# Block 1's statistics behind block 0's scaling, turns' copies ahead of others, and six drains in the prologue

## The chip, the core and the metric

One core of a Trainium2 chip. Times are device microseconds (us) of a whole execution. Each kernel was run several times in rounds, each round beside the kernel before on the same chip; a profile is one further execution, whose span (first to last instruction) is 1.6 to 1.8 us below the timed figure.

## The reference, cut to what matters

```python
x = A_x                                   # 2048 tokens x 512, bf16
xn = layernorm(x)                         # over the 512, no gain, no bias
qkv = xn @ wqkv                           # 32 heads of 16
a = softmax(mask(q k^T / 4)) v            # causal, window of 256 keys
out = x + a @ wo + ((xn @ w_gate) * (xn @ w_up)) @ w_down
```

The tokens are worked in four chunks of 512, a chunk in four blocks of 128. The scores are the matmuls of q k^T; PE does them in 76 batches, and the exponentials of the softmax follow on ACT. Of the work, only that of chunk 0, the first 17 us, is touched.

## The kernel before: what the change and the argument touch

The kernel is written out by a list scheduler of its own: while it is built, it simulates the engines with a table of durations and emits each instruction when its turn comes. V is DVE, A is ACT, G is POOL, P is PE. Cuts are marked.

```python
class Kernel:
    HOLD = 0.1
    # ... prologue: loads, constants, then
        nc.gpsimd.memset(self.V[0][:, :, :, 16:18], 1.0)
        self.keep_busy(42, 0)             # 42 dummy matmuls on PE

    def loop(self):                       # the next copy, scaling, ...
        # ... for every waiting op o and every engine e that may do it
        key = (at + (0.3 if e == "A" and len(o.on) > 1 else 0.0)
               + (self.HOLD if o.rank and now0 else 0.0), o.rank, t)
        # ... the smallest key is done next; now0: no score batch yet

    def choose(self):                     # the next work of PE
        # ... for the first four dense pieces d, t = when it could start
        t -= 0.3 * (d.name.startswith("turn") and t <= now + 0.25)
        # ... the smallest t wins

    def first_chunk(self):
        land = (3.4, 3.95, 7.7, 9.6)      # landings of x, blocks 0 to 3
        wv, wk, wq = 5.9, 7.3, 9.3        # landings of the weights
        # per block b: statistics (DVE), root (ACT), reciprocal and scaling (DVE),
        # "turn": four transposes on PE and a copy xT out of PSUM (rank 0),
        # then V, K, Q projections (16 matmuls each) and copies out of PSUM (rank 1)
```

Block 1's statistics are cut into two halves: the first when x has landed, the second behind the scaling of block 0.

The softmax here doesn't subtract the row's maximum and nothing guards it: scores larger than these inputs give would overflow.

## Time and profile before

| | before |
|---|---|
| median of 3 runs when I predicted | 265.97 us |
| median of the later runs | 265.6 to 265.7 us |
| PE busy in the span of 264.0 us | 98% |
| first real work of PE (V of block 0) | 6.29 us |
| first scores | 17.33 us |
| last matmul starts | 260.22 us |

The lines are in the prediction. Below, the tail is the time from the start of the last matmul to the end of the program.

### The profile page before, as it was taken

Reading aid. Unit: us, or ns where it says so; the run is one execution under the profiler, and the core shown is the slowest. Engines: PE = TensorE matmul, PEld = TensorE weight load, DVE = VectorE, ACT = ScalarE, POOL = GpSimd, SP = SyncE. Lnnn points to the kernel's source line nnn. Section 1 sums busy time; section 2 is a strip of 40 time slices with the busy share of each in tenths; the row PEclk is TensorE's granted clock in tenths of the full one; section 3 lists DMA queues with packets and bytes.
Section 4 is the critical chain, followed back from the end, with each engine's and each line's share of the span. In section 5 each row is a group of like instructions: output and inputs, shape, how many; then the busy total and the mean of one; then the engine's idle time right before and its main releaser. Section 6 shows DMA issues by size and latency. Waiting matters only on the chain.

```text
span 264.0 us, 8009 instructions
## 1 busy us (share of the span) xinstructions
PE 259.4 (98%) x3456; PEld 131.9 (50%) x3456; DVE 190.6 (72%) x368; ACT 165.0 (63%) x122; POOL 119.7 (45%) x272
## 2 busy tenths in 40 slices
PE   8999999999999999999999999999999999999994
PEld 7974444554444354455534354546535353545462
DVE  4999886978996548777997467786946268786504
ACT  3457576768776766687776767677777676572000
POOL 1406655475175635427084736437081828255000
PEclk9999999999999999999999999999999999999999
DMA  6999910000002200000005200000000100000002
GB/s 219 381 374 350 215 22 1 2 0 2 4 2 59 64 22 22 0 2 2 2 0 83 62 22 0 4 2 0 2 2 22 40 4 22 2 0 2 0 2 81
DMA packets 17251, 13.88 MB, mean 53 GB/s; under 512 B 7104, under 2 KB 17216, under 8 KB 17216
## 3 DMA queue, kind: packets, MB, share of 16 engines
q1 hardware_dynamic: 16784, 13.05, 18.0%
q8 instruction: 27, 0.44, 0.7%
q10 hardware_dynamic: 432, 0.33, 0.4%
q14 instruction: 8, 0.07, 0.1%
HBM read 9.70 MB, written 2.10 MB: 45 GB/s over the span
## 4 chain that ended last, share of the span: by engine, by line
PE 96%; DMA 2%; DVE 1%; ACTq 0%; issue 0%
PE M L207 72%; PE S L215 9%; PE M L245 7%; PE M L689 6%; DMA x<-in_A_x_dram 1%; DMA out_dram<-xn 1%; PE M L624 1%; PE S L207 1%; DVE xn L783 1%; DVE st L591 0%; ACTq L149 0%; DVE xn L273 0%; PE M L197 0%; DVE rs L603 0%
## 5 line engine op out<-in xcount | busy, mean ns | idle before, releaser
L498 ACT ACTIVATE P<-S 128x2048 bf16<-128x2048 f32 x76 | 140.9, 1854 | 57.1 <-PE S L215 50.5
L224 POOL TENSOR_SCALAR_AFFINE_SELECT P<-P 64x256 bf16<-64x256 bf16 (+1 forms) x248 | 112.6, 456 | 112.9 <-ACT P L498 100.7
L207 PE MATMUL M<-xnT,Wg 128*128 128x512 bf16 x224 | 57.7, 380 | 0.0
L207 PE MATMUL M<-xnT,Wu 128*128 128x512 bf16 x224 | 57.7, 380 | 0.0
L207 PE MATMUL M<-Wd,hT 128*128 128x512 bf16 (+1 forms) x224 | 51.8, 373 | 0.0
L741 DVE TENSOR_TENSOR hT<-M,gsb 128x512 bf16<-128x512 f32 x56 | 38.0, 678 | 8.4 <-PE M L207 8.1
L207 PEld LDWEIGHTS <-hT 128*128 128x128 bf16 x238 | 21.7, 98 | 23.4 <-issue 2.1
L207 PEld LDWEIGHTS <-Wu 128*128 128x128 bf16 x224 | 20.5, 98 | 24.8 <-issue 1.8
L207 PEld LDWEIGHTS <-Wg 128*128 128x128 bf16 x224 | 20.2, 98 | 24.3 <-issue 2.4
L203 DVE CAST gsb<-M 128x512 bf16<-128x512 f32 x41 | 28.1, 686 | 5.3 <-PE M L207 4.9
L207 PE MATMUL M<-xnT,Wqkv 128*128 128x128 bf16 (+1 forms) x224 | 30.3, 288 | 0.0
L215 PE MATMUL S<-Q,K 32*128 32x320 bf16 (+3 forms) x720 | 30.0, 254 | 0.0
L534 DVE STREAM_TRANSPOSE at<-M 128x512 f32<-128x512 f32 x32 | 21.3, 698 | 9.7 <-PE M L245 9.6
L215 PEld LDWEIGHTS <-K 32*128 32x128 bf16 x720 | 11.9, 92 | 31.8 <-issue 30.9
L230 DVE TENSOR_TENSOR P<-P,masks 128x512 int16<-128x512 int16 x56 | 22.6, 410 | 7.1 <-ACT P L498 7.1
L207 PEld LDWEIGHTS <-Wqkv 128*128 128x128 bf16 x224 | 15.9, 98 | 10.6 <-issue 1.5
L783 DVE TENSOR_TENSOR y<-M,x 128x512 bf16<-128x512 f32 x12 | 8.2, 687 | 16.5 <-PE M L207 16.3
L245 PE MATMUL M<-P,V 64*17 64x320 bf16 (+4 forms) x1440 | 19.5, 252 | 0.0
L245 PEld LDWEIGHTS <-V 64*17 64x17 bf16 x1440 | 17.1, 86 | 3.2 <-issue 1.3
L284 DVE TENSOR_SCALAR K<-M,own 128x512 bf16<-128x512 f32 x24 | 17.1, 743 | 2.1 <-PE M L207 2.1
L207 PE MATMUL M<-Wo,OT 128*128 128x512 bf16 (+1 forms) x64 | 16.6, 374 | 0.0
L689 PE MATMUL M<-Wqkv,xnT 128*64 128x256 bf16 x256 | 15.5, 274 | 0.0
(51 smaller groups left out, 138.0 us busy)
## 6 DMA issues: line engine op xcount, KB each, us to landing
Wg<-in_B_w_gate_dram SPq DMA_DIRECT2D x2, 896.0 KB, 10.2
Wu<-in_B_w_up_dram SPq DMA_DIRECT2D x2, 896.0 KB, 11.9
out_dram<-y SPq DMA_DIRECT2D x12, 128.0 KB, 1.7
Wqkv<-in_A_wqkv_dram SPq DMA_DIRECT2D x2, 512.0 KB, 6.1
x<-in_A_x_dram SPq DMA_DIRECT2D x1, 1024.0 KB, 13.6
Wd<-in_B_w_down_dram SPq DMA_DIRECT2D x2, 512.0 KB, 11.6
Wd<-in_B_w_down_dram SPq DMA_DIRECT2D x2, 384.0 KB, 8.7
Wqkv<-in_A_wqkv_dram SPq DMA_DIRECT2D x2, 256.0 KB, 3.5
```

Of the source, the lines that this page charges most:

```text
L203: self.nc.vector.tensor_copy(out=out, in_=in_)
L207: self.nc.tensor.matmul(ps, lhsT=a, rhs=b, start=first and n == 0, stop=last and n == len(pairs) - 1)
L215: self.nc.tensor.matmul(self.S[:, e, 64 * at:64 * (at + m)], lhsT=self.K[U % 3][rows, c, j].rearrange("p l t -> p (l t)"), rhs=self.Q[T % ...
L224: self.nc.gpsimd.affine_select(out=v, in_=v, pattern=[[0, 4], [0, n], [sign, 64]], base=0, fill=0.0, compare_op=ALU.is_gt if kind else ALU ...
L230: self.nc.vector.tensor_tensor(out=v, in0=v, in1=m, op=ALU.bitwise_and)
L245: self.nc.tensor.matmul(banks[lane][32 * e:32 * e + 17, 64 * q:64 * (q + m)], lhsT=self.V[U % 3][rows, j, 4 * c + e, 0:17], rhs=P[rows, e, ...
L284: self.nc.vector.tensor_scalar(out=out, in0=in_, scalar1=own, scalar2=None, op0=ALU.mult)
L498: ex = self.op(f"exp{g}", {"A": (took + 0.06, took + 0.18)}, [o], lambda e: self.nc.scalar.activation(out=P[:, :, 0:hi], in_=self.S[:, :, ...
L534: t = self.op(f"tr{v}", {"V": (0.63, 0.71)}, [o] + ts, lambda e, par=par: nc.vector.transpose(out=self.at[:, :, par, :], in_=self.M[banks[ ...
L689: self.nc.tensor.matmul(self.M[i][64 * lane:64 * lane + 64, 256 * jj:256 * jj + 256], lhsT=self.xnT[T % 2][:, k, tok], rhs=w[:, lane], sta ...
L741: x = self.op(f"u{T}.{f}", {"V": PSUM_COPY["V"]}, [o, ("gate", T, f)], lambda e: self.nc.vector.tensor_tensor(out=self.hT[T % 2][:, f, :], ...
L783: self.nc.vector.tensor_tensor(out=keep["y"][:, cols], in0=self.M[i][:, cols], in1=self.x[:, t, cols], op=ALU.add)
```

## The change

The intent: start block 0's chain of statistics, root, reciprocal, scaling and turn sooner, since half of block 1's statistics stood in its way; keep copies of turns, which PE waits for, ahead of other copies out of PSUM (HOLD); give the scheduler landings and starts nearer to what the chip shows; and add one DVE and five POOL drains, whose purpose is not written down. (A drain is an instruction that computes nothing. In the trace the first of them lasts until the engine's work ahead of it is done: 0.25 us on DVE, 0.79 on POOL.)

```diff
--- before.py
+++ after.py
@@ -89,7 +89,7 @@
     PACE = 2.9
     SHARE = 1.0
     FEED = 0.1
-    HOLD = 0.1
+    HOLD = 0.3
 
     def __init__(self, live=True):
         self.live = live
@@ -186,6 +186,9 @@
         nc.vector.tensor_copy(out=self.own[:, 1:2], in_=podd[:])
         nc.vector.tensor_scalar(out=self.own[:, 0:1], in0=podd[:], scalar1=0, scalar2=None, op0=ALU.is_equal)
         nc.gpsimd.memset(self.V[0][:, :, :, 16:18], 1.0)
+        nc.vector.drain()
+        for _ in range(5):
+            nc.gpsimd.drain()
         self.keep_busy(42, 0)
 
 
@@ -258,9 +261,9 @@
                                          compare_op=ALU.is_gt if kind else ALU.is_ge, channel_multiplier=-sign)
 
     def i_stats(self, t, mv):
-        st = self.work.tile([128, 2, 6], F32, tag="st", name="st")
-        self.nc.vector.bn_stats(out=st[:, 0, :], in_=self.x[:, t, :])
-        self.nc.vector.bn_aggr(out=mv[:, t % 4, :], in_=st[:, 0, :])
+        st = self.work.tile([128, 6], F32, tag="st", name="st")
+        self.nc.vector.bn_stats(out=st[:], in_=self.x[:, t, :])
+        self.nc.vector.bn_aggr(out=mv[:, t % 4, :], in_=st[:])
         self.nc.vector.tensor_scalar(out=self.ve[:, t:t + 1], in0=mv[:, t % 4, 1:2], scalar1=1e-5, scalar2=None,
                                      op0=ALU.add)
 
@@ -288,8 +291,8 @@
     def run(self):
         if self.live:
             self.prologue()
-        self.now, self.mode = 5.4, "D"
-        self.free = {"V": 3.0, "A": 4.5, "G": 3.0, "S": 6.0}
+        self.now, self.mode = 4.8, "D"
+        self.free = {"V": 3.0, "A": 3.4, "G": 3.0, "S": 6.0}
         self.waiting, self.log, self.idle = [], [], []
         self.banks = [0.0] * 4
         self.s_free, self.p_free = 0.0, [0.0] * self.PBUFS
@@ -575,28 +578,20 @@
 
     def first_chunk(self):
 
-        land = (3.4, 3.95, 7.7, 9.6)
-        wv, wk, wq = 5.9, 7.3, 9.3
+        land = (3.4, 4.6, 7.9, 9.7)
+        wv, wk, wq = 5.2, 7.5, 9.35
         nc = self.nc
         roots = []
         for b in range(4):
             keep = {}
 
-            halves = 2 if b == 1 else 1
-
-            def bn(e, n, b=b, keep=keep, halves=halves):
-                if n == 0:
-                    keep["st"] = self.work.tile([128, 2, 6], F32, tag="st", name="st")
-                cols = slice(n * 512 // halves, (n + 1) * 512 // halves)
-                nc.vector.bn_stats(out=keep["st"][:, n, :], in_=self.x[:, b, cols])
-                if n == halves - 1:
-                    nc.vector.bn_aggr(out=self.mv[0][:, b, :], in_=keep["st"][:, 0:halves, :])
-
-            deps = [land[b]]
-            for n in range(halves):
-                took = (0.72 if halves == 1 else 0.38) + (0.14 if n == halves - 1 else 0)
-                s = self.op(f"st{b}", {"V": (took, took + 0.04)}, deps, lambda e, n=n, bn=bn: bn(e, n), rank=0.5)
-                deps = [self.at_["ap", 0, 0], s] if b == 1 else deps
+            def bn(e, b=b, keep=keep):
+                keep["st"] = self.work.tile([128, 6], F32, tag="st", name="st")
+                nc.vector.bn_stats(out=keep["st"][:], in_=self.x[:, b, :])
+                nc.vector.bn_aggr(out=self.mv[0][:, b, :], in_=keep["st"][:])
+
+            deps = [land[b]] + ([self.at_["ap", 0, 0]] if b == 1 else [])
+            s = self.op(f"st{b}", {"V": (0.86, 0.90)}, deps, bn, rank=0.5)
             s = self.op(f"sq{b}", {"A": (0.24, 0.25)}, [s], lambda e, b=b: nc.scalar.activation(
                 out=self.ve[:, b:b + 1], in_=self.mv[0][:, b, 1:2], func=ACT.Sqrt, bias=self.eps[:]), rank=0)
             roots.append(s)
```

## The prediction

> **What bounds the kernel now.** I read the page first (its busy times), then who waited for whom on PE, then the instructions in order of time for the first 18 us, and last the table by stretches.
>
> The page's busy times:
>
> ```profile
> PE 259.4 (98%) x3456; PEld 131.9 (50%) x3456; DVE 190.6 (72%) x368; ACT 165.0 (63%) x122; POOL 119.7 (45%) x272
> ```
>
> The waits of PE:
>
> ```profile
> PE M L197 <- PEq L817: 0.8, 1, 0.8
> PE M L624 <- DVE xn L273: 0.2, 1, 0.2
> ```
>
> PE is the bound, with hardly a recorded wait. Cut at 17.3 us, the table by stretches gives PE 11.03 of 11.10 us (6.2 to 17.3) and 232.70 of 232.70 us (17.3 to 250). So the time is: when PE's real work begins, plus its work, plus waits inside it, plus the tail. The change touches only work before 17.3 us. Instructions in order of time there (start, duration, engine, line, operation):
>
> ```profile
> 3.41 0.69 DVE L591 BATCH_NORM_STATS2 st<-x 128x6 f32<-128x512 bf16 x1 [1.47 <-DMA x<-in_A_x_dram]
> ...
> 4.35 0.29 ACT L600 ACTIVATE ve<-mv,eps 128x1 f32<-128x1 f32 x1 [1.12 <-DVE mv L593]
> 4.60 0.43 DVE L591 BATCH_NORM_STATS2 st<-x 128x6 f32<-128x256 bf16 x1 [0.29 <-DMA x<-in_A_x_dram]
> 4.95 0.15 DVE L603 RECIPROCAL rs<-ve 128x1 f32<-128x1 f32 x1
> 5.13 0.60 DVE L273 TENSOR_SCALAR xn<-x,mv,rs 128x256 bf16<-128x256 bf16 x2
> ...
> 5.65 0.42 DVE L591 BATCH_NORM_STATS2 st<-x 128x6 f32<-128x256 bf16 x1
> ...
> 6.10 0.21 DVE L593 BATCH_NORM_AGGREGATE mv<-st 128x2 f32<-128x12 f32 x1
> ...
> 6.29 1.06 PE L689 MATMUL M<-Wqkv,xnT 128*64 128x256 bf16 x16
> 6.40 0.30 ACT L600 ACTIVATE ve<-mv,eps 128x1 f32<-128x1 f32 x1
> ...
> 7.40 0.40 PE L624 MATMUL M<-ident,xn 128*128 128x128 bf16 x4
> ...
> 7.63 2.92 PE L207 MATMUL M<-xnT,Wqkv 128*128 128x128 bf16 x48
> ...
> 10.58 0.40 PE L624 MATMUL M<-ident,xn 128*128 128x128 bf16 x4
> ...
> 10.81 1.95 PE L207 MATMUL M<-xnT,Wqkv 128*128 128x128 bf16 x32
> ...
> 11.70 0.16 DVE L603 RECIPROCAL rs<-ve 128x1 f32<-128x1 f32 x1
> 11.90 0.41 DVE L273 TENSOR_SCALAR xn<-x,mv,rs 128x512 bf16<-128x512 bf16 x1
> ...
> 12.60 0.39 PE L624 MATMUL M<-ident,xn 128*128 128x128 bf16 x4
> ```
>
> L624 is the four transposes ("turn") of a block of 128 rows, L689 its V projection, L207 here its K and Q projections, 16 matmuls each. To see waits inside a busy PE I take starts, not ends. From 10.81 to 12.60 there are 32 matmuls with no wait: 55.9 ns each, so 0.89 us for a projection and 0.22 for a turn. The 48 from 7.63 to 10.58 should take 2.68 and take 2.95: 0.27 of waiting (0.08 before K of block 1, 0.19 before turn 2). V of block 0 takes 0.85 and turn 1 starts 1.11 after it: 0.26 of waiting. After turn 2 I find none until 17 us. All that this stretch has to give is 0.5 us of waits plus an earlier start.
>
> **What the Trainium skill says.** Perfetto Trace Analysis, section Tensor Engine Instruction (MATMUL, LD_WEIGHTS): the end shown for a matmul is an estimate. The trace agrees: a 128-column matmul is shown with 216 to 219 ns while the next starts 56 ns later; hence the reading by starts. TensorE: Matmul & The Clock Gate, section Step-by-step: 55.6 ns measured between matmuls of 128 columns; here 55.9, so that stretch is at its floor. VectorE: DVE Perf Modes, section The DRAIN you can't avoid: a boilerplate DRAIN is about 12 ns. That the added drains cost as little is my estimate from it; no view of this trace shows a drain's duration. Runtime: NRT & Kernel Launch, section Instruction fetch mechanics: instructions come in 16 KiB blocks, mostly hidden. Added drains shift the block borders of DVE and POOL; the DMA queue of instructions moves 27 such pieces here and I see no PE wait near one, so I give this no gain.
>
> **The change part by part.**
>
> *Drains.* DVE's last prologue work starts at 1.79 and its next at 3.41; POOL idles from 1.8 to 7.7. Six drains at 12 ns fit in both holes: 0.
>
> *Statistics of block 1 behind the scaling of block 0.* ACT's root for block 0 ends at 4.35 + 0.29 = 4.65, and the reciprocal usually follows within 0.03 (blocks 1 and 3: 6.70 to 6.73, 11.67 to 11.70). Here it starts at 4.95 because the half statistics of 4.60 hold DVE. Without them: reciprocal 4.68, scaling 4.68 + 0.18 = 4.86 instead of 5.13. Turn 0 and V of block 0 come 0.27 earlier (6.02). But the whole statistics of block 1 now follow the two scalings: they start at 4.86 + 0.52 = 5.38, and the aggregate 0.725 later (as 3.41 to 4.14) at 6.10: exactly where it is now. Its 0.18 instead of 0.21 and an ACT that has finished its copies let the root start at 6.32 instead of 6.40. Turn 1 thus starts at about 7.32 instead of 7.40. V of block 0 ends at 6.87 and PE waits 0.44 instead of 0.26. Then the K weights bind: issued at 1.83 with 5.7 us to landing they are there at 7.54, so K of block 0 starts at 7.60 instead of 7.63. The 0.27 won at the head is worth 0.03.
>
> *Copies of turns ahead.* The kernel orders its instructions itself, by a list scheduler with its own durations, while it is built. HOLD 0.3 lets the copy of a turn, and scaling, pass others out of PSUM. I followed its rules by hand through block 3, for the order alone; the times are the trace's. On DVE the masks' memset (7.35) moves behind, so V's copy starts at 7.17, turn 1's copy at 7.75 instead of 8.14, statistics of block 2 at 8.08 instead of 8.46 (x block 2 lands 2.33 + 5.6 = 7.93). K's copy (0.635 to the next) still goes ahead of the reciprocal of block 2: 9.54; scaling 9.73, done 10.14. PE: K0 7.60, K1 8.50 (its 0.08 of waiting gone), Q0 9.41 (its weights land 2.88 + 6.5 = 9.38), turn 2 at 10.30 instead of 10.58: 0.28 ahead.
>
> Then the order of PE changes. The scheduler prefers a turn if it expects it within 0.25 us of PE coming free. Its sums from turn 2's start to turn 3 being ready are 0.28 + 0.22 + 0.31 + 0.22 + 0.54 = 1.57; to PE free after Q of block 1, plus 0.25, they are 0.28 + 1.05 + 0.25 = 1.58. So it now puts turn 3 before K of block 2, by 0.007; now it misses by some 0.05. On the chip, statistics of block 3 start at 10.06, aggregate 10.78, root 10.99, reciprocal 11.32, scaling 11.52 done 11.93, turn 3 at 11.99 (0.06 from scaling to turn, as at 5.53, 7.40 and 10.58). Q of block 1 ends at 10.30 + 0.22 + 0.89 = 11.42: a new wait of 0.57. Then turn 3 and K of block 2 are done at 11.99 + 0.22 + 0.89 = 13.10, against 12.82 now (they have changed places). The sum is -0.28 (head, K1, turn 2) + 0.57 (new wait) = +0.28 after rounding.
>
> From there the scheduler's clock is shifted nearly as a whole, so I expect the same work in nearly the same order, 0.28 later: 265.97 + 0.28 = 266.25; I say 266.2.
>
> **The rivals.**
>
> First, the order stays (K of block 2, then turn 3). For it: my margin of 0.007 is thin, and one slip in forty sums by hand upsets it. Then K of block 2 starts at 11.42, turn 3 at 12.31, and 0.28 is kept: 265.7. I give it three in ten.
>
> Second, later flips. The planned start of each score batch moves by a quarter us, near ties decide which of DVE and ACT copies a gate, and where V groups go. A switch into a score batch shows as 0.31 instead of 0.22 between matmul starts, so 0.1 each, and a few more or fewer move the end by 0.1 to 0.5 either way. For it: 76 batches; against it: the shift is uniform and PE has no wait of another kind after 17 us.
>
> Third, the drains do more than I think, by moving where DVE and POOL fetch. The author took the trouble of choosing five. PE does not wait for POOL in this trace, so there is nothing to win, but a slip could cost up to an us: 267.
>
> Fourth, the whole head gain arrives: 0.27 + 0.45 of waits gone, 265.3. Against it: turn 1 hangs on block 1's statistics, which do not move, and K's weights land at 7.54.
>
> **Range and chances.** Middle 266.2, rivals from 265.3 to 267.0; the three times of before already spread from 265.8 to 266.6. So 265.4 to 267.0. Two per cent is 5.3 us, over five times the largest rival: within 2% 0.98, 0.01 either side.
>
> **What would show it.** Right: reciprocal of block 0 near 4.68, V of block 0 near 6.02, block 1's aggregate still near 6.10, turn 1 near 7.32, L207 from 7.60, turn 2 near 10.30, then only 16 matmuls, turn 3 near 12.0 after some half us of wait, first scores (17.33 now) near 17.6, and an end as much later. Wrong: 32 matmuls between turns 2 and 3; a turn 1 well before 7.2; a PE wait over 0.3 us after 17 us; or first scores moved one way and the end another.

## The result, and the profile after

| | before | after |
|---|---|---|
| median, first comparison (6 runs each) | 265.71 us | 265.97 us |
| median, second comparison (11 and 6 runs) | 265.60 us | 265.95 us |
| ratio, first | | 1.0008 (0.9990 to 1.0027) |
| ratio, second | | 1.0005 (0.9987 to 1.0022) |

A ratio is the mean time of one kernel's runs over that of the other's of the same rounds, so not quite the ratio of the medians quoted. The verdict is "same"; the medians are 0.26 and 0.35 us apart, where the prediction had 0.28 more. The intervals of the ratios reach from -0.3 to +0.7 us, so the times alone do not confirm it.

The busy times of the page of the changed kernel:

```profile
PE 259.9 (98%) x3456; PEld 132.3 (50%) x3456; DVE 190.5 (72%) x367; ACT 165.3 (62%) x122; POOL 120.0 (45%) x272
```

DVE has one instruction fewer (the half statistics), PE the same 3456 matmuls. The changed kernel's instructions in order of time (L590 statistics, L591 aggregate, L598 reciprocal, L276 scaling, L200 PE's dummy matmuls, L619 turns, L684 V, L210 K and Q, L218 scores; the bracket is idle time before it and what ended it):

```profile
4.71 0.16 DVE L598 RECIPROCAL rs<-ve 128x1 f32<-128x1 f32 x1 [0.36 <-ACT ve L595]
...
5.76 0.63 PE L200 MATMUL M<-const-bfloat16-1.0 128*128 128x128 bf16 x4
6.15 0.18 DVE L591 BATCH_NORM_AGGREGATE mv<-st 128x2 f32<-128x6 f32 x1
6.32 1.20 PE L684 MATMUL M<-Wqkv,xnT 128*64 128x256 bf16 x16
...
7.45 0.40 PE L619 MATMUL M<-ident,xn 128*128 128x128 bf16 x4
...
7.89 2.85 PE L210 MATMUL M<-xnT,Wqkv 128*128 128x128 bf16 x48
...
10.61 0.40 PE L619 MATMUL M<-ident,xn 128*128 128x128 bf16 x4
10.85 1.06 PE L210 MATMUL M<-xnT,Wqkv 128*128 128x128 bf16 x16
...
12.40 0.40 PE L619 MATMUL M<-ident,xn 128*128 128x128 bf16 x4 [0.50 <-DVE xn L276]
12.63 3.74 PE L210 MATMUL M<-xnT,Wqkv 128*128 128x128 bf16 x64
```

Read three things. The reciprocal comes at 4.71 instead of 4.95 and the aggregate of block 1 at 6.15, not moved. Only 16 matmuls stand between turns 2 and 3, and turn 3 waits: the order changed as worked out. Counted by starts, as the view's 0.50 is measured from modelled ends, the wait is 0.66. But the head of this execution gained nothing: V of block 0 starts at 6.32, K at 7.89.

I then set the 3456 matmuls of the two traces side by side. They come in the same order but for turn 3 and K of block 2, which have changed places. Behind these every start is 0.70 us later, to a few ns, for 200 us; near 213 us this becomes 0.86 in one step; and the end of the program is only 0.55 later. So there are three places to explain: the head (+0.70), a step near 213 (+0.16), and a tail that is shorter (3.44 instead of 3.75 us from the start of the last matmul to the end). The prediction had +0.28 for the first and nothing for the other two.

### The profile page after: what moved, and what is told of

Same layout as the page of the kernel before. It is cut to its first block, busy times and chain, and to the rows that moved or that the text cites. A ratio compares the mean times of both kernels' runs of the same rounds, so it can differ in the third digit from the quotient of the medians.

```text
span 264.5 us, 8015 instructions
## 1 busy us (share of the span) xinstructions
PE 259.9 (98%) x3456; PEld 132.3 (50%) x3456; DVE 190.5 (72%) x367; ACT 165.3 (62%) x122; POOL 120.0 (45%) x272
## 4 chain that ended last, share of the span: by engine, by line
PE 95%; DVE 2%; ACT 1%; DMA 1%; issue 0%; ACTq 0%
PE M L210 70%; PE S L218 9%; PE M L248 7%; PE M L684 6%; PE M L200 2%; ACT P L501 1%; DMA out_dram<-xn 1%; PE S L210 1%; DVE xn L778 1%; DVE st L590 0%; PE M L619 0%; DVE xn L276 0%; DVE V L206 0%; DVE K L287 0%; DVE mv L591 0%
## 5 line engine op out<-in xcount | busy, mean ns | idle before, releaser
L210 PE MATMUL M<-xnT,Wg 128*128 128x512 bf16 x224 | 57.7, 380 | 0.0
L210 PE MATMUL M<-xnT,Wu 128*128 128x512 bf16 x224 | 57.7, 380 | 0.0
L210 PE MATMUL M<-Wd,hT 128*128 128x512 bf16 (+1 forms) x224 | 51.8, 373 | 0.0
L210 PEld LDWEIGHTS <-hT 128*128 128x128 bf16 x238 | 21.6, 98 | 23.4 <-issue 2.1
L210 PEld LDWEIGHTS <-Wu 128*128 128x128 bf16 x224 | 20.5, 98 | 24.8 <-issue 1.8
L210 PEld LDWEIGHTS <-Wg 128*128 128x128 bf16 x224 | 20.2, 98 | 24.3 <-issue 2.4
L210 PE MATMUL M<-xnT,Wqkv 128*128 128x128 bf16 (+1 forms) x224 | 30.3, 288 | 0.0
L218 PE MATMUL S<-Q,K 32*128 32x320 bf16 (+3 forms) x720 | 30.1, 254 | 0.1
L218 PEld LDWEIGHTS <-K 32*128 32x128 bf16 x720 | 12.0, 92 | 31.9 <-issue 30.9
L210 PEld LDWEIGHTS <-Wqkv 128*128 128x128 bf16 x224 | 15.8, 98 | 10.8 <-issue 1.5
L287 DVE TENSOR_SCALAR K<-M,own 128x512 bf16<-128x512 f32 x23 | 16.4, 743 | 2.6 <-PE M L210 2.6
L210 PE MATMUL M<-Wo,OT 128*128 128x512 bf16 (+1 forms) x64 | 16.6, 374 | 0.0
L684 PE MATMUL M<-Wqkv,xnT 128*64 128x256 bf16 x256 | 15.6, 275 | 0.0
```

The costliest lines, as they stand in the source:

```text
L210: self.nc.tensor.matmul(ps, lhsT=a, rhs=b, start=first and n == 0, stop=last and n == len(pairs) - 1)
L218: self.nc.tensor.matmul(self.S[:, e, 64 * at:64 * (at + m)], lhsT=self.K[U % 3][rows, c, j].rearrange("p l t -> p (l t)"), rhs=self.Q[T % ...
L287: self.nc.vector.tensor_scalar(out=out, in0=in_, scalar1=own, scalar2=None, op0=ALU.mult)
L684: self.nc.tensor.matmul(self.M[i][64 * lane:64 * lane + 64, 256 * jj:256 * jj + 256], lhsT=self.xnT[T % 2][:, k, tok], rhs=w[:, lane], sta ...
```

## The experiments

Twelve runs followed, in groups that shared a chip and the runs of the kernel before. Of each profile I give: "wk", when the K weights landed; "turn 2"; "wait 3", PE's wait ahead of turn 3 by starts; "scores", the first ones; "scores to scores", from the first to the last score batch's matmuls; "tail", from the start of the last matmul to the end. They are from the starts of single instructions and the landing events in the trace.

| kernel | wk | turn 2 | wait 3 | scores | scores to scores | tail | time, median | ratio to before |
|---|---|---|---|---|---|---|---|---|
| before | 7.54 | 10.58 | 0 | 17.33 | 219.84 | 3.75 | 265.71 | |
| c1 before again | 7.37 | 10.58 | 0 | 17.33 | 219.84 | 3.73 | 265.71 | 1.0003 |
| changed | 7.84 | 10.61 | 0.66 | 18.03 | 220.00 | 3.44 | 265.97 | 1.0008 |
| c2 changed again | 8.26 | 11.10 | 0.37 | 18.21 | 220.00 | 3.28 | 265.95 | 1.0005 |
| c3 order back | 6.61 | 10.32 | 0 | 17.21 | 219.99 | 3.32 | 265.40 | 0.9984 |
| c4 drains alone | 7.43 | 10.39 | 0 | 17.14 | 219.83 | 3.25 | 265.19 | 0.9980 |
| d1 one DVE, three POOL | 7.55 | 10.68 | 0 | 17.43 | 219.84 | 3.61 | 265.51 | 0.9994 |
| d2 five POOL only | 7.84 | 10.65 | 0 | 17.39 | 219.84 | 3.61 | 265.35 | 0.9986 |
| d3 changed, no drains | 6.62 | 10.21 | 0.67 | 17.62 | 220.00 | 3.70 | 266.15 | 1.0017 |
| d4 order back, borders | 7.34 | 10.32 | 0 | 17.21 | 219.83 | 3.25 | 265.37 | 0.9980 |
| f1 turn 3 first, in before | 7.32 | 10.36 | 0.67 | 17.79 | 219.84 | 3.77 | 266.52 | 1.0033 |
| f2 changed, HOLD 0.1 | 6.94 | 10.44 | 0 | 17.95 | 219.84 | 3.53 | 266.11 | 1.0012 |
| f3 order, Q first | 7.44 | 10.40 | 0 | 17.36 | 219.84 | 4.08 | 266.09 | 1.0018 |
| g1 the same, two DVE drains | 7.31 | 10.39 | 0 | 17.33 | 219.84 | 3.25 | 265.30 | 0.9981 |

Beside the kernel before, medians of 265.60 (c), 265.70 (d), 265.61 (f) and 265.72 us (g).

### c1 and c2: what is noise

No edit: the two kernels as they are.

> The kernel before against itself, as a measure of what is noise. Ratio 1.000 within 0.002 either way. Profile: how far the landings of the weights and the moment at which PE's matmul spacing falls from 107 to 56 ns differ from one execution to the next. If [...]the clock gate is what made the changed kernel's V of block 0 late (6.32), that moment differs between the two profiles of this same kernel by up to some us; if it comes from the change, it is near 5.1 again. Waits of PE ahead of turns 1 and 2 near 0.26 and 0.19, none ahead of turn 3.

> The changed kernel as it is. Ratio 1.001, between 0.999 and 1.003. Profile: PE waits 0.5 to 0.7 us ahead of turn 3 again (my theory: the new order). The 0.16 us wait of a score batch near 213 us, which only one profile shows, is gone if it is noise and there again if the order makes it. If the K weights land at 7.55 instead of 7.84 as in the one profile, K of block 0 starts near 7.6.

The kernel before against itself gave 1.0003, with 0.2% either way: the time alone cannot settle a quarter us, the traces can. Two things in the head differ from one execution of the same kernel to the next. PE's spacing fell from 107 to 56 ns at 5.04 us in one profile of the kernel before and only after 6.18 in the other; over all fourteen profiles the fall lies between 4.0 and 6.7. And the K weights land between 6.61 and 8.26. In the second profile of the changed kernel the clock was early and V of block 0 came at 5.96 (6.02 predicted), but the weights were late:

```profile
7.24 0.40 PE L619 MATMUL M<-ident,xn 128*128 128x128 bf16 x4 [0.22 <-DVE xn L276]
8.31 2.95 PE L210 MATMUL M<-xnT,Wqkv 128*128 128x128 bf16 x48 [0.67 <-DMA Wqkv<-in_A_wqkv_dram]
```

So the V of 6.32 in the first profile was a late clock (its four dummy matmuls of 5.76 stand at 107 ns and PE does them in order), and the K of 7.89 and 8.31 were late weights. My expectation that the step near 213 us was perhaps noise fell: it is there again (220.00 from scores to scores against 219.84).

### c3 and f1: the order

```diff
-                t -= 0.3 * (d.name.startswith("turn") and t <= now + 0.25)     # changed kernel
+                t -= 0.3 * (d.name.startswith("turn") and t <= now + 0.20)     # c3
```

```diff
-                t -= 0.3 * (d.name.startswith("turn") and t <= now + 0.25)     # kernel before
+                t -= 0.35 * (d.name.startswith("turn") and t <= now + 0.32)    # f1
```

> The changed kernel with K of block 2 ahead of turn 3 again; by the kernel's own plan nothing else on PE moves. My theory (the new order turns the head's gain into a wait): the wait of 0.6 before turn 3 is gone, first scores about 0.55 to 0.65 earlier than in the changed kernel in a like execution, time 0.5 us below it (ratio to before 0.998 to 0.9995). Rival (the head's gain never reaches turn 2, and the time after it makes no difference because the score batches are paced): same time as the changed kernel within 0.1 us.

> The kernel before with turn 3 moved ahead of K of block 2, the order that the change brings, and nothing else of the change (a copy of Q and of turn 3 change engines with it). My theory: scaling of block 3 is done at 12.31 in the kernel before whatever PE does, Q of block 1 ends at 11.70, so PE waits 0.6 to 0.7 us ahead of turn 3 and all that follows is 0.6 to 0.7 later: ratio 1.0020 to 1.0030, time 266.3. Rival (the wait is an artefact of late weights in the profiles of the changed kernel): no wait over 0.2 there, ratio 1.000.

With the order back, c3 ran 0.55 us below the changed kernel on the same chip, as expected: its slowest run (265.61) is below the other's fastest (265.67). PE in c3 (L619 turns, L210 projections):

```profile
10.32 0.40 PE L619 MATMUL M<-ident,xn 128*128 128x128 bf16 x4
10.55 1.95 PE L210 MATMUL M<-xnT,Wqkv 128*128 128x128 bf16 x32
12.34 0.39 PE L619 MATMUL M<-ident,xn 128*128 128x128 bf16 x4
12.71 2.84 PE L210 MATMUL M<-xnT,Wqkv 128*128 128x128 bf16 x48
```

There are 32 matmuls between the turns again and no wait ahead of turn 3; but Q of block 2 starts 0.37 behind turn 3 instead of 0.22. The 0.15 are a new wait, by the times for a copy of Q that held a PSUM bank: it stands behind the scaling of block 3 on DVE and runs from 11.97 to 12.65, and Q of block 2 starts at 12.71. That HOLD put the copy there is my reading; no run shows it. The order put alone into the kernel before makes it worse by about its wait:

```profile
12.16 0.40 PE L624 MATMUL M<-ident,xn 128*128 128x128 bf16 x4 [0.51 <-DVE xn L273]
```

That is 0.67 by starts, with K weights at 7.32, so late weights are not needed for it: they lessen it (0.37 in c2), as PE then comes later and DVE goes on. f1's time is 0.9 above before, more than the 0.67; its profile was 0.46 later at the first scores against the one of before, with a head that began 0.2 earlier. The interval of its ratio (0.45 to 1.3 us) holds both figures; the rest I leave open.

### c4: the drains alone

```diff
         nc.gpsimd.memset(self.V[0][:, :, :, 16:18], 1.0)
+        nc.vector.drain()
+        for _ in range(5):
+            nc.gpsimd.drain()
         self.keep_busy(42, 0)
```

> The kernel before with the six drains alone. My theory: 0, ratio 1.000 within 0.002, first statistics still at 3.4 and the first scores at 17.3, since both engines idle there. Rival (the drains move where DVE and POOL fetch instructions): a time off by over 0.3 us, with PE waits after 17 us that the kernel before does not have.

My theory fell. The drains alone are 0.4 us faster than the kernel before (0.9980, 0.9963 to 0.9997), and the rival is wrong too in its detail: PE has no new wait. The gain that the drains bring is in the tail, 3.25 instead of 3.75. The trace's records of the sequencers, which the views leave out, show where (starts in us; instructions numbered per engine from 0 in the order of the records):

```
kernel before                                  drains alone
DVE  446 waits for barrier      262.998        447 waits for barrier      262.746
DVE  447 DRAIN                  263.467        448 DRAIN                  262.856
POOL 323 clears semaphores      263.137        328 clears semaphores      262.885
POOL 324 DRAIN                  263.557        329 DRAIN                  263.015
DVE, last: passes last barrier  263.924        passes last barrier        263.225
```

From the barrier wait to the DRAIN DVE takes 0.47 before and 0.11 with drains; POOL takes 0.42 and 0.13 for its step. The last barrier waits for both. In all four profiles without drains (the kernel before twice, d3, f1) it is number 447 of DVE and number 324 of POOL that comes late, whatever else was changed. A theory followed: these are the first instructions of a new block of instructions, and drains ahead put another instruction there.

The tail also holds the landing of the last output, which takes 1.55 to 1.74 us from its issue in all profiles but f3's. Counted from that landing, the end comes 1.29 to 1.31 us later in the four profiles without drains, and 0.85 to 0.86 later in c4 and in both profiles of the changed kernel. So the six drains bring 0.43 to 0.46 us; what the tails differ by beyond that is the landing.

In c4's profile the head, too, is 0.19 earlier. That I do not put down to the drains: in this execution x block 1 landed at 4.39 instead of 4.58, so that its half statistics were out of the way of block 0's reciprocal sooner (4.75 instead of 4.95), and d1, with drains and a landing at 4.58, has no such gain, while f1, without drains and with a landing at 4.31, has it.

### d1, d2 and d3: borders, part by part

```diff
-        for _ in range(5):       # c4
+        for _ in range(3):       # d1
```

```diff
-        nc.vector.drain()        # c4; without this line: d2
```

d3 is the changed kernel without its six drains.

> The kernel before with one DVE drain and three POOL drains instead of five. From the four profiles with and without drains: at the end of the program the time from the last matmul's start to the end is 3.73 to 3.76 us without drains and 3.25 to 3.44 with them, because one DVE and one POOL instruction behind the last barrier start 0.3 to 0.4 us late, always at the same count of the engine's instructions (DVE number 447, POOL number 324). Theory (a border between blocks of instructions is crossed there, and drains ahead move it to an instruction that waits anyway): three drains are too few, POOL's number 324 is then still behind the barrier's wait, so the late start is at an earlier instruction and the tail stays near 3.6 to 3.75, time within 0.15 us of before; DVE's late instruction is gone. Rival (drains help in some other way, at the head): time like that of the six drains, 0.3 to 0.45 us below before, tail near 3.25.

> The kernel before with the five POOL drains, without the DVE one. Theory of the border: POOL's late start is gone, DVE's number 447 still starts 0.36 late behind the barrier, and the last barrier waits for whichever is later, so of the 0.45 us only 0.1 to 0.2 come: tail 3.55 to 3.65, time 0.1 to 0.2 us below before. Rival: the whole 0.4, tail near 3.25.

> The changed kernel without its drains. Theory: late starts of DVE number 447 (or a neighbour) and POOL number 324 are back, tail 3.6 to 3.75 instead of 3.28 to 3.44, time 266.3 (0.3 to 0.45 us above the changed kernel, ratio to before 1.0015 to 1.003). The wait of a score batch of 0.16 us near 213 us stays, as it belongs to ACT's number 191, which drains on DVE and POOL do not move. Rival (drains do nothing): time of the changed kernel.

In all three the late instructions and the tails came out as the theory of the border says. The times were further off: d1 is 0.19 below before (within 0.15 expected), d2 0.35 (0.1 to 0.2), d3 only 0.2 above the changed kernel (0.3 to 0.45). Their intervals are too wide to read more into that. With three POOL drains, number 324 is a semaphore update right behind the barrier's wait, and it starts 0.38 behind it, where the same pair is 0.08 apart in c4: tail 3.61. With POOL's five alone, DVE's number 447 is late as before (0.49): tail 3.61. The changed kernel without drains has both late again, tail 3.70 and a time 0.2 above the changed kernel. That fits the choice of five over three: with five, number 324 is a select (at 240.80 us in c4), far ahead of the wait, where a delay costs nothing. Four, which would put number 324 on the barrier's wait itself, was not run.

d3 is also a test of my arithmetic on the head without late weights, as its K weights landed at 6.62. Its PE (L616 turns, L207 projections, L215 scores):

```profile
7.29 0.40 PE L616 MATMUL M<-ident,xn 128*128 128x128 bf16 x4 [0.23 <-DVE xn L273]
7.53 2.84 PE L207 MATMUL M<-xnT,Wqkv 128*128 128x128 bf16 x48
10.21 0.39 PE L616 MATMUL M<-ident,xn 128*128 128x128 bf16 x4
10.43 1.06 PE L207 MATMUL M<-xnT,Wqkv 128*128 128x128 bf16 x16
11.99 0.40 PE L616 MATMUL M<-ident,xn 128*128 128x128 bf16 x4 [0.51 <-DVE xn L273]
...
17.62 0.40 PE L215 MATMUL S<-Q,K 32*128 32x256 bf16 x8
```

Turn 1 at 7.29 (7.32 predicted), turn 2 at 10.21 (10.30), turn 3 at 11.99 (11.99), first scores 0.29 later than before (0.28). The size of that gain at turn 2 is in part owed to x, which landed sooner in d3 than in the profile before (block 1 at 4.37 instead of 4.58); the part on the prediction comes back to it.

### d4: ACT's border

The step near 213 us begins with a late exponential on ACT. ACT in the changed kernel:

```profile
209.01 1.88 ACT L501 ACTIVATE P<-S 128x2048 bf16<-128x2048 f32 x1 [0.74 <-PE S L218]
211.90 1.88 ACT L501 ACTIVATE P<-S 128x2048 bf16<-128x2048 f32 x1 [1.01 <-POOL P L227]
```

The bracket blames POOL. But the wait instruction just ahead was through at 211.53, and in the pairs around it the exponential starts 0.08 behind it, not 0.37. By the records it is ACT's number 191, and 447 is 191 + 256. In the kernel before, number 191 is a wait for scores that lasts until 213.43 anyway, so nothing is seen. The changed kernel has one ACT wait more in chunk 0, which moved an exponential there. c3, with the order back, has that wait and the step too (its exponential of 211.07 is 0.36 behind its wait), so the order of PE does not make the step.

A second late exponential puts the spacing of the borders at 128 instructions rather than 256. Number 63 of ACT starts 0.40 behind its wait in the changed kernel (66.68 us); in the kernel before the same exponential has another number, and starts 0.14 behind it. Numbers 63 and 191 are late in the five profiles in which they are exponentials right behind a wait (the changed kernel twice, c3, d3, f2); no other operation of ACT right behind a wait starts 0.21 to 0.7 us after it in any of the fourteen. The trace of DMA packets agrees: on one queue of instructions pieces of 8 KB move, and one moves 0.6 to 0.7 us behind each late start that stands alone: 212.53 behind ACT's 211.90, 263.99 behind POOL's 263.28 in d1, 264.20 behind DVE's 263.56 in d2. The late instruction does not wait for that piece, which moves after it. What it does wait for, no run shows.

```diff
-        nc.vector.drain()              # c3
+        for _ in range(3):
+            nc.vector.drain()
         for _ in range(5):
             nc.gpsimd.drain()
+        nc.scalar.drain()
```

> K of block 2 ahead of turn 3 as in the earlier run, three DVE drains instead of one, and one drain on ACT. Theory: ACT's number 191 is then an instruction that waits anyway, so the exponential near 211 us no longer starts 0.29 us late and the 0.15 us wait of the score batch behind it is gone; DVE's number 447 falls on the barrier's wait, so the end is 0.1 us shorter than in the run with the order alone: 0.2 to 0.3 us below it, about 265.15, ratio to before 0.998. Rival (the late exponential comes from POOL's selects, not from ACT's own instructions): the wait near 213 stays and the time is within 0.1 of the run with the order alone.

ACT in the kernel before, and then in d4, the same exponentials:

```profile
210.91 1.88 ACT L498 ACTIVATE P<-S 128x2048 bf16<-128x2048 f32 x1 [0.72 <-POOL P L224]
```

```profile
208.19 1.88 ACT L503 ACTIVATE P<-S 128x2048 bf16<-128x2048 f32 x1 [0.74 <-PE S L220]
210.79 1.88 ACT L503 ACTIVATE P<-S 128x2048 bf16<-128x2048 f32 x1 [0.72 <-POOL P L229]
```

One drain on ACT took the delay away: 0.72 again, 219.83 from scores to scores against 219.99 in c3, no step. The view still names POOL, which it did all along. The time, 265.37, is only 0.03 below c3 and not the 0.2 to 0.3 expected; its profile span is 0.22 below. The runs fall in two groups (264.98 and 265.07; 265.37 to 265.41), and five runs cannot say more.

### f2: what HOLD is for

```diff
-    HOLD = 0.3
+    HOLD = 0.1
```

> The changed kernel with HOLD at 0.1 as before, so without the part that sends copies of turns ahead; by the kernel's plan K of block 2 is then ahead of turn 3, and on DVE the first K copy of block 1 goes ahead of turn 2's copy. My theory of what HOLD is for: turn 2's copy then ends near 12.05 instead of 11.4, and PE waits about 0.6 ahead of K of block 2 instead of 0.5 to 0.7 ahead of turn 3: time like the changed kernel, ratio 1.000 to 1.002. Rival (HOLD is what brought the new order and nothing else): no wait over 0.2 us between turn 2 and the first scores, ratio 0.998 like the run with the order back.

As expected, the wait changes places. PE in f2, K of block 2:

```profile
12.33 1.05 PE L210 MATMUL M<-xnT,Wqkv 128*128 128x128 bf16 x16 [0.60 <-DVE xnT L206]
```

Without the larger HOLD a copy of K goes ahead of turn 2's copy on DVE, which then starts at 11.87, and PE waits 0.76 by starts for it. So HOLD pays in this order of things: c3, with the same order of PE and HOLD 0.3, has the first scores at 17.21 and f2 at 17.95. What undid it in the changed kernel was the place of turn 3. (The tail, 3.53, is longer than the changed kernel's because other wait instructions put DVE's number 447 on the DRAIN behind the barrier again.)

### f3 and g1: a version to beat both

```diff
-    HOLD = 0.3
+    HOLD = 0.2
-        nc.vector.drain()
+        for _ in range(3):             # g1: range(2)
+            nc.vector.drain()
-                t -= 0.3 * (d.name.startswith("turn") and t <= now + 0.25)
+                t -= 0.3 * (d.name.startswith("turn") and t <= now + 0.20)
-                    ... c=4)), rank=1)       # copy of Q out of PSUM, chunk 0
+                    ... c=4)), rank=0.9)
```

> A version to beat both: the changed kernel with K of block 2 ahead of turn 3, HOLD 0.2, the Q copies of chunk 0 ahead of K copies that are ready at the same moment (so Q of block 0 goes to ACT at once and its PSUM bank is free when Q of block 2 wants it), and three DVE drains. The run with order and borders still had 0.15 of waiting ahead of Q of block 2; theory: that wait was for the bank that Q of block 0 held, and is gone. Turn 2 near 10.3 when the weights are not late, Q of block 2 at 12.55 instead of 12.71, first scores near 17.05, tail 3.25, no late exponential near 211 (ACT has the order of before): 265.0, ratio to before 0.997. Rival (drains alone are all that can be had, as the head hangs on the landings): 265.2 to 265.4, ratio 0.998 to 0.9985.

This failed twice. The wait ahead of Q of block 2 did not go, it is 0.21: by the times, the bank that Q wants is now that of K of block 1, whose copy runs to 12.80 on DVE. And the tail was 4.08, by the outputs alone: from the last landing to the end it has 0.85, like c4. The last two outputs landed late; the view of the outputs from 260.5 us on says for f3:

```profile
DMA to landing us min/median/max: 1.7/2.3/2.4
```

Its third DVE drain had put DVE's number 447 on the last instruction ahead of the final barrier, and in the trace an 8 KB piece of instructions moves at 261.73, 0.65 us behind the issue of the last output; in the other profiles it moves 1.14 us or more behind it, when the outputs have nearly landed. So I ran the same with two drains:

> The last version with two DVE drains instead of three, nothing else. In its profile the last two outputs took 2.35 and 2.40 us to land where every other profile has 1.55 to 1.74, an 8 KB piece of instructions was fetched at 261.73 while they were on their way (the others fetch it after 262.0), and DVE's number 447 was its last instruction before the final barrier. Theory: the border there makes DVE fetch just then, and the fetch holds the outputs up. With one drain fewer number 447 is the wait behind it: outputs land in 1.6 us again, from the last matmul to the end 3.25 instead of 4.08, time 0.7 to 0.8 us lower, 265.3, ratio to before 0.9985. The wait of 0.2 us ahead of Q of block 2, for the bank of K of block 1, stays. Rival (slow outputs have another cause, or were chance): tail and time as in the last version, 266.0.

```profile
DMA to landing us min/median/max: 1.6/1.6/1.7
```

That is g1: tail 3.25, and 0.79 below f3. One drain too many cost twice what the right ones bring. That the fetch itself held the outputs up fits the times of the pieces; that the drain's place decides is shown, the way in which it does is not.

c4, d4 and g1 (0.9980, 0.9980, 0.9981 of before, where the changed kernel has 1.0005 and 1.0008) are ahead of both kernels and cannot be told apart. The simplest is the kernel before with the drains alone.

## Why the prediction was right or wrong, point by point

- **PE bounds, and only the head counts.** Right for PE's order (no other exchange in 3456 matmuls), wrong in that the tail and one exponential at 211.90 us count as well.
- **Statistics moved: the head comes 0.27 earlier, block 1 does not move.** Right: the reciprocal came at 4.71 and the aggregate at 6.15 (4.68 and 6.10 predicted, x having landed 0.03 later). That the gain dies at turn 1 and at the K weights was right; I had taken their landing as fixed at 7.54, and it wanders by more than all of the gain (6.61 to 8.26). I also took x block 1's landing as fixed, and whether the move pays hangs on it. Counted from the landing of x block 0, turn 1 starts 3.94 to 4.03 us later in the eight profiles with the statistics moved. In the six with the halves it starts 4.01 to 4.17 later where block 1 lands 1.17 to 1.24 behind block 0 (before, c1, d1), but only 3.76 to 3.78 where it lands 0.90 to 0.97 behind (c4, d2, f1). So at turn 1 the move wins up to 0.2 us in the first case, which was the profile I predicted from, and loses about 0.2 in the second.
- **Turn 2 earlier by 0.28.** Right in size when the weights are not late: 10.21 in d3, 10.32 in c3 and d4, against 10.58. But with block 1 landing early c4 and f1 have 10.39 and 10.36 with neither the moved statistics nor HOLD 0.3, so of the 0.28 less than 0.2 is shown to be the change's. In the two profiles of the changed kernel they were late, and it was not earlier.
- **Turn 3 ahead of K of block 2, a wait of 0.57.** Right. The margin of 0.007 was not checked; c3 shows that the plan expects turn 3 between 0.20 and 0.25 us after PE comes free. The wait measured 0.66 and 0.37 in the changed kernel and 0.67 in d3.
- **"Six drains at 12 ns fit in both holes: 0."** This is the step that failed. They do fit, but what they bring is not in the hole. They take 0.43 to 0.46 us from the tail (from the last landing to the end 1.29 to 1.31 without, 0.86 in the changed kernel). I had seen that they shift the borders of blocks, had looked only at PE's waits, and had not looked behind the last matmul at all. The 27 pieces that I looked at are by their number PE's own (its 6925 records over 256 are 27); DVE and POOL have the 8 KB pieces of another queue. The third rival ("the drains do more than I think, by moving where DVE and POOL fetch") named the mechanism, with the sign wrong: "nothing to win".
- **Nothing later.** Wrong by 0.16: one more wait instruction on ACT put an exponential on ACT's border.
- **The sum.** +0.28 predicted, +0.26 and +0.35 between the medians, +0.21 and +0.13 by the ratios, each give or take 0.45. That the number came so near is partly luck. From d3 and the tails, +0.29 head, +0.16 ACT's border and -0.44 tail make about 0; against c4 (first scores at 17.14), where block 1 landed about as in d3, the head is +0.48 and the sum +0.2. Late weights and a late clock added 0.41 and 0.59 to the head in the two profiled executions, which are both slower than the median of their runs; how much they add to the other runs no profile shows. So the missed term (drains) was made up in part by ACT's border, which I did not have, and perhaps by late weights.

## What to carry to other kernels

When a kernel is bound by one engine and has no waits left on it, look at its two ends: the landings that start it, and the barrier behind its last instruction, where here every engine's own delay was exposed. A start 0.3 to 0.4 us late that stuck to the same number of an engine's instruction stream in all variants was here a border of that stream; shift it by an instruction or two to where the engine waits anyway, and check the result, as one too many can cost more. And when a planner moves work ahead to save a wait, follow which near tie in its rules the saved time now tips.

## What the Trainium skill lacked or had wrong

- Runtime: NRT & Kernel Launch, section Instruction fetch mechanics, calls the cost of a border "mostly hidden". It is 0.28 to 0.38 us where the engine has nothing to wait for (ACT 211.90, DVE 263.47, POOL 263.56 us), and 0.43 to 0.46 us of this program's end; the page does not say how to see it or shift it. Its blocks of 16 KiB and 256 instructions fit PE here (27 pieces of 16 KB; 6925 records over 256 are 27). They do not fit ACT, which is late at its numbers 63 and 191, 128 apart; the pieces that move behind late starts of ACT, DVE and POOL are of 8 KB, which is not on that page.
- VectorE: DVE Perf Modes, section The DRAIN you can't avoid, gives 12 ns for a boilerplate drain and nothing for one that a program adds. The added drains show 34 to 41 ns each on POOL behind the first and 10 to 19 on DVE (d4, f3, g1), and the first on each engine lasts until the work ahead is done (0.79 us on POOL, 0.25 on DVE). I used 12; it made no difference.
- TensorE: Matmul & The Clock Gate, section What you observe, puts the fall of the spacing at about 4 us into the matmuls, give or take 0.5. Here, with the first matmul at 0.84, it fell between 4.0 and 6.7 in fourteen profiles, so 3.1 to 5.9 us in. The section What's actually happening lays the scatter to a window that runs free. That the moment differs between executions of one kernel agrees (5.04 and 6.18 us for the kernel before); the window itself no run here shows.
- No page has how far the landing of a load wanders: the K weights, issued at 1.82 in each, landed from 6.61 to 8.26 us.
